# More zero matmuls before the first attention products, and the first expert's work handed out two rounds later

## The chip, the cores and the metric

The kernel runs on one core of a Trainium2 chip. The metric is the device time of one execution in microseconds (us). Engines are named as in the profile: PE is the matrix engine, PEld its weight load, DVE the vector engine, ACT the scalar engine, POOL GpSimd, SP the engine that issues most DMAs.

## What is computed

A linear attention with a decaying state gives x of 3072 tokens by 384, and a mixture of 8 experts with a balanced gate follows it.

```python
for t in range(S):                                  # B=4, H=8, S=768, D=48
    cur = einsum('bhd,bhe->bhde', u[None] * kt, vt)
    y[:, :, t] = einsum('bhd,bhde->bhe', rt, state + cur)
    state = w[None, :, :, None] * state + einsum('bhd,bhe->bhde', kt, vt)
...
logits = x @ w_gate                                 # N=3072, D=384, E=8
P = np.exp(logits - logits.max())
for _ in range(8):
    P /= P.sum(1, keepdims=True) + 1e-09
    P /= P.sum(0, keepdims=True) + 1e-09
    P *= N / E
for e in range(E):
    h = np.maximum(x @ w1[e], 0.0)                  # 384 -> 1024
    out += P[:, e:e + 1] * (h @ w2[e])              # 1024 -> 384
```

## The kernel before

**Start.** Tables of powers of the decay are made on DVE. Meanwhile PE multiplies zeros (`spin`, tile `pz`, 128x512 in fp16; nobody reads the result) and then transposes the tables (`pt_tab`). Every engine next loads a flag and branches (lines 450 and 451): if a decay lies outside a safe span, a slow path runs, a long piece of code that lies between this branch and everything that follows. Here the branch jumps over it.

**Attention rounds.** The 3072 tokens are 24 tiles of 128. A loop over rounds i = 0 to 26 writes the instructions of all engines in program order; each engine executes its own list in that order. In round i: loads for tile i+4 (SP), scaled copies `rp`, `kp` for tile i+2 (POOL, DVE), products `rk` (POOL), transposes `prT`, `pkT` of tile i+1 (PE, copied out by ACT), then `run`, then scores `pA` of tile i (PE), their masked copy `at` (DVE), the state update `pu`, `S` (PE, DVE, POOL), then `run`, then transposes `px` of tile i-2, the output `py` of tile i-1 with its scaling `x`, `xm`, `xs` (DVE, ACT), then `prepare`, and the gate products `pg` of tile i-3 with `logits` (DVE). The PSUM tiles of all of these share one tag with 4 buffers, so that `pA` of a round can start only when the `logits` or `x` of earlier tiles have been read.

**Side work.** Two lists are emptied a piece at a time between these stages. `prepare` pops one piece of `side`: expert 0's weights w1 and then w2 are split into a high and a low fp16 half, by 3 maxima (`amax`, DVE, tile `wm`), `reduce_max`, `across` (the maximum over partitions: a transpose `pmax_w` on PE, DVE's `mt_w` and `md_w`, a tiny matmul), `scale`, and 4 steps of `high` (ACT) and `low` (DVE, tile `ws`). `run(n)` calls `prepare` once and then pops n pieces of `units`. Units are expert 0's matmuls: for each of the first four tiles two `g1_chunk` (36 matmuls 128x128, tile `phc`), then four `g2_half` (12 matmuls, tile `po`). Two become available at the end of each of the rounds 2 to 5, the four `g2_half` at the end of round 5, and the next sixteen at the end of round 9. A round calls `run(1)`, `run(2 if i % 3 < 2 else 1)` and one `prepare`: so 3 pieces of side work and up to 3 or 2 units. Units then fall in rounds 3 (2), 4 (2), 5 (2), 6 (3) and 7 (3), and none is left for rounds 8 and 9.

**After.** Rounds 10 to 26, a loop over ticks that empties the rest of `units`, and 14 half experts.

Of the kernel before, what the change touches and what calls it, by code (L numbers as in the profile page):

```python
# [32 lines left out]
def rwkv_sinkhorn_moe(  # L33
# [25 lines left out]
    KC = DM // P  # L59
# [28 lines left out]
    def part(home, dtype, at, shape):  # L88

        n = 1  # L90
        for s_ in shape:
            n *= s_
        x_ = home if home.dtype == dtype else home.bitcast(dtype)
        x_ = x_[:, at : at + n]
        if len(shape) == 1:
            return x_
        names = "abcd"[: len(shape)]
        return x_.rearrange(
            f"p ({' '.join(names)}) -> p {' '.join(names)}", **{c_: s_ for c_, s_ in zip(names[1:], shape[1:])}
        )  # L100
# [21 lines left out]
    def pow2_scale(m, inv, s, down):  # L122
        V.tensor_scalar(inv, m, 1e-30, down, op0=ALU.max, op1=ALU.mult)
        V.tensor_single_scalar(
            inv.bitcast(I32), inv.bitcast(I32), EXP_MASK, op=ALU.bitwise_and
        )
        V.reciprocal(s, inv)


    def over_partitions(m, n, pool, tag, name):  # L130

        pt = pool.tile([P, TB], F32, tag=tag, name=f"pmax_{name}")
        T.transpose(pt[:n, :P], m, ident)
        mt = sm.tile([P, 1], F32, tag="mt", name=f"mt_{name}")
        V.tensor_reduce(mt[:n], pt[:n, :P], axis=AX.X, op=ALU.max)
        md = sm.tile([P, 2], F32, tag="md", name=f"md_{name}")
        V.tensor_scalar_mul(md[:n, :n], ident[:n, :n], mt[:n])
        yield pt[:, 2 * P : 2 * P + n]
        T.matmul(pt[:, 2 * P : 2 * P + n], ones[:n, :], md[:n, :n], start=True, stop=True)
        yield pt[:, 2 * P : 2 * P + n]  # L140


    def split_weights(e, r1, r2, home):
        w1h = part(home, F16, 0, (KC, F))
        w1l = part(home, F16, KC * F, (KC, F))
        w2h = part(home, F16, 2 * KC * F, (FC, DM))
        w2l = part(home, F16, 2 * KC * F + FC * DM, (FC, DM))
        isw = const.tile([P, 2], F32, name=f"isw_{e}")
        sw = sm.tile([P, 2], F32, tag="sw", name=f"sw_{e}")
        m = sm.tile([P, 2 * KC], F32, tag="wm", name=f"wm_{e}")  # L150
        ma_ = [sm.tile([P, 1], F32, tag=f"wma{j}", name=f"wma_{e}_{j}") for j in range(2)]
        res = {}
        pieces = []
        for raw, wh, wl, j in ((r1, w1h, w1l, 0), (r2, w2h, w2l, 1)):
            fl = [x.rearrange("p c f -> p (c f)") for x in (raw, wh, wl)]
            n = fl[0].shape[1] // KC

            def amax(i, fl=fl, j=j, n=n):
                V.tensor_reduce(
                    m[:, j * KC + i : j * KC + i + 1], fl[0][:, i * n : (i + 1) * n],  # L160
                    axis=AX.X, op=ALU.max, apply_absolute_value=True,
                )

            def reduce_max(j=j):
                V.tensor_reduce(ma_[j], m[:, j * KC : (j + 1) * KC], axis=AX.X, op=ALU.max)

            def across(j=j):
                res[j] = over_partitions(ma_[j], 1, ps1, "ph", f"w{e}_{j}")
                next(res[j])

            def scale(j=j):
                pow2_scale(next(res[j]), isw[:, j : j + 1], sw[:, j : j + 1], 0.25)

            def high(i, fl=fl, j=j, n=n):
                sl = slice(i * n, (i + 1) * n)
                S_.activation(fl[1][:, sl], fl[0][:, sl], AF.Copy, scale=sw[:, j : j + 1])

            def low(i, fl=fl, j=j, n=n):
                sl = slice(i * n, (i + 1) * n)
                V.scalar_tensor_tensor(  # L180
                    fl[2][:, sl], fl[0][:, sl], sw[:, j : j + 1], fl[1][:, sl],
                    op0=ALU.mult, op1=ALU.subtract,
                )

            steps = [lambda i=i, f=amax: f(i) for i in range(KC)] + [reduce_max, across, scale]
            for i in range(KC + 1):
                fs = [lambda i=i, f=high: f(i)] if i < KC else []
                fs += [lambda i=i, f=low: f(i - 1)] if i else []
                steps.append(lambda fs=fs: [f() for f in fs])
            pieces += steps  # L190
        return (w1h, w1l, w2h, w2l, isw), pieces
# [57 lines left out]
    def whole(gen):  # L249
        for _ in gen:  # L250
            pass
# [25 lines left out]
    def spin(n):  # L277
        pz = ps2.tile([P, TB], F32, tag="po", name="pz")
        for _ in range(n):
            T.matmul(pz, zeros[:, :P], zeros, start=True, stop=True)  # L280
# [4 lines left out]
    def load_part(tt, nm, src):  # L285
        b, c = divmod(tt, NCHB)
        t_ = ld.tile([P, H, D], F32, tag=nm + "n", name=f"{nm}n_{tt}", bufs=5 if nm == "v" else 3)
        Q.dma_start(t_, src[b, :, c * C : (c + 1) * C, :].rearrange("h t d -> t h d"))
        loads.setdefault(tt, {})[nm] = t_

    def load_chunk(tt):
        for nm, src in (("r", r), ("k", k), ("v", v)):
            load_part(tt, nm, src)
# [23 lines left out]
        xf[2].rearrange("p t (a q) -> p t a q", q=HP),  # L317
        unit[:, :1, 1:].unsqueeze(1).broadcast_to([P, TTH, 2 * KC, HP]), 0.0,
    )
    spin(16)  # L320
    wsafe = ac.tile([P, NPAIR], F32, name="wsafe")
    good = ac.tile([P, NPAIR], F32, name="good")
    V.tensor_scalar(wsafe, wt, W_MAX, W_MIN, op0=ALU.min, op1=ALU.max)
# [125 lines left out]
    with tc.high_priority():  # L449
        bad = nc.values_load(flag.bitcast(I32), min_val=0, max_val=0x3F800000)  # L450
        with tc.If(bad > 0):
            with tc.tile_pool(name="scratch", bufs=1, space=bass.MemoryType.DRAM) as scratch:
                scan_channels(scratch)

    load_part(0, "v", v)
    Q.dma_start(
        ub.rearrange("p h d -> p (h d)"),
# [19 lines left out]
    def gate_max():  # L477
        V.tensor_reduce(wgm, wg, axis=AX.XY, op=ALU.max, apply_absolute_value=True)

    def gate_across():  # L480
        res = over_partitions(wgm, 1, ps1, "ph", "wg")
        next(res)
        return res

    def gate_split(res):
        pow2_scale(next(res), iswg, swg, 0.25)
        S_.activation(wgh, wg, AF.Copy, scale=swg)
        V.scalar_tensor_tensor(wgl, wg, swg, wgh, op0=ALU.mult, op1=ALU.subtract)
# [6 lines left out]
    def prep(tt):  # L495
        ld_ = loads[tt]
        G.tensor_tensor(rp_[tt % 2][:, :, :D], ld_["r"], rt4, op=ALU.mult)
        V.tensor_tensor(kp_[tt % 3][:, :, :D], ld_["k"], kt4, op=ALU.mult)
        st[tt] = {}

    def bonus_dot(tt):
        ld_ = loads[tt]
        rk = at2.tile([P, H, D], F32, tag="rk", name=f"rk_{tt}")
        G.tensor_tensor(rk, ld_["r"], ld_["k"], op=ALU.mult)
        G.tensor_tensor(rk, rk, ub, op=ALU.mult)
        st[tt]["rk"] = rk
# [108 lines left out]
    def prepare():  # L615
        if side:
            side.pop(0)()

    def run(n):
        prepare()  # L620
        for _ in range(n):
            if units:
                units.pop(0)()

    W, side = split_weights(0, *raws, ws1)
    prep(0)
    prep(1)
    stage_b(0)
    bonus_dot(0)
    for i in range(NTT + 3):  # L630
        if i == 2:
            gate_max()
        if i == 3:
            gate_split(gate_res)
        if i + 2 < NTT:
            if i + 4 < NTT:
                load_chunk(i + 4)
            if i == 0:
                Q.dma_start(raws[1], w2[0].rearrange("(c p) d -> p c d", p=P))
            prep(i + 2)  # L640
        if i + 1 < NTT:
            bonus_dot(i + 1)
            stage_b(i + 1)
        run(1)
        if i < NTT:
            bonus(i)
            if ("S", i) in st:
                st[i]["S"] = st.pop(("S", i))
            stage_c(i)
        run(2 if i % 3 < 2 else 1)  # L650
        if i == 2:
            gate_res = gate_across()
        if 2 <= i <= NTT + 1:
            stage_e(i - 2)
        if 1 <= i <= NTT:
            stage_d(i - 1)
        prepare()
        if 3 <= i:
            stage_f(i - 3)
        done = i - 2  # L660
        if 0 <= done < TPB:
            units += [lambda t=done, g=g: g1_chunk(t, g, W) for g in range(2)]
            if done == TPB - 1:
                units += [lambda t=t: whole(g2_half(0, t, 0, W)) for t in range(TPB)]
                pend = [(0, t, 1) for t in range(TPB)]
        elif TPB <= done < NTT and done % TPB == TPB - 1:
            tb = done // TPB
            for j in range(2):
                g1 = [lambda fc=fc, tb=tb: g1_unit(tb, fc, W) for fc in range(j * FHC, (j + 1) * FHC)]
                g2 = [lambda a=a: whole(g2_half(*a, W)) for a in pend]  # L670
                units += merged(g1, g2)
                pend = [(tb, t, j) for t in range(TPB)]
# [448 lines left out]
    for s in range(NS):  # L1121
        tasks = stage_tasks(s)
        for g in range(NG):
            for j in range(2):
                for n, nxt in enumerate(g1_slots(s, g, j)):
# [3 lines left out]
                    i = j * NPR + n  # L1129
# [37 lines left out]
```

## Time and profile before

| | us |
|---|---|
| median of 3 runs | 1611.08 |
| the runs | 1612.73, 1610.4, 1611.08 |
| the profiled execution | 1613.47 |
| its span, first to last instruction | 1611.8 |
| PE busy in the span | 1569.0 (97%) |

The page gives one execution. A share of busy time is a mean over stages, so the stretch that the change touches, the first 117 us, is read by itself: in windows (busy time of each engine in given stretches), in the timeline (each engine's instructions in order, with what ended an idle time) and in the list of waits. Rounds are told apart by PE's `prT`, with which PE begins one: round 1 at 24.31, 2 at 31.20, 3 at 40.44, 4 at 57.47, 5 at 67.84, 6 at 78.60, 7 at 90.98, 8 at 102.17, 9 at 109.39, 10 at 116.55 us.

### The profile page before, as it was taken

To read this page: it belongs to the slowest core of one execution; us is meant where nothing else is said; L and a number is where in the kernel's file an instruction comes from. 1 tells how busy PE (TensorE), PEld (TensorE's weight loads), DVE (VectorE), ACT (ScalarE), POOL (GpSimd) and SP (SyncE) were. 2 spreads that over 40 slices of the span, in tenths; PEclk is the share of its full clock that TensorE was granted. 3 is DMA by queue.
4 is the path that set the end of the run, shared out by engine and by line. 5 is a ranking of instruction groups with operands and counts; after the bars stand their busy time and mean duration, and the time that the engine had idled before them with its cause. 6 is when DMAs were issued, how large, how long until landed. Compare 5 with 4: busy or idle time off the path is not lost.

```text
span 1611.8 us, 24273 instructions
## 1 busy us (share of the span) xinstructions
PE 1569.0 (97%) x9438; PEld 906.7 (56%) x9438; DVE 1019.6 (63%) x1706; ACT 665.9 (41%) x1174; POOL 580.1 (36%) x688
## 2 busy tenths in 40 slices
PE   7899999789999999999999999999999999999998
PEld 5887777344455555555555555555555555555555
DVE  6665554787766666666666666666666665656554
ACT  3232232243444445453545454444444443535320
POOL 7455542665020242424242424333232424242200
PEclk7999999889999999999999999999999999999999
DMA  7242320202022556565665656564545454545433
GB/s 183 50 90 64 85 60 31 74 35 84 30 93 55 103 74 122 84 123 83 113 99 75 122 80 127 84 113 56 97 52 98 55 95 54 97 55 89 60 90 130
DMA packets 159547, 135.54 MB, mean 84 GB/s; under 512 B 83906, under 2 KB 153667, under 8 KB 159427
## 3 DMA queue, kind: packets, MB, share of 16 engines
q0 software_dynamic: 44928, 61.36, 29.6%
q1 hardware_dynamic: 114288, 72.58, 15.6%
q8 instruction: 75, 1.23, 0.3%
q14 instruction: 46, 0.37, 0.1%
q10 hardware_dynamic: 210, 0.00, 0.0%
HBM read 53.69 MB, written 80.22 MB: 83 GB/s over the span
## 4 chain that ended last, share of the span: by engine, by line
PE 92%; DVE 5%; POOL 1%; issue 0%; ACT 0%; DMA 0%; SPq 0%; DVEq 0%; POOLq 0%
PE po L29 46%; PE bZ L29 11%; PE bY L29 11%; PE bB L29 4%; PE bA L29 4%; PE ph L29 4%; PE py L29 3%; PE bC L29 2%; PE pA L29 2%; PE pu L29 1%; PE phc L29 1%; DVE xv L29 1%; PE prT L29 1%; DVE ws L29 1%; PE pkT L29 1%; DVE hb L29 1%
## 5 line engine op out<-in xcount | busy, mean ns | idle before, releaser
L29 PE MATMUL po<-ws,hb 128*128 128x384 f16 x4608 | 893.9, 327 | 1.2 <-DVE cs L29 1.2
L29 PEld LDWEIGHTS <-hb 128*128 128x128 f16 x4824 | 459.7, 98 | 383.9 <-issue 5.2
L29 POOL DMA_DIRECT2D accd<-stg x288 | 250.4, 870 | 699.9 <-ACT stg L29 681.5
L29 PEld LDWEIGHTS <-ws 128*128 128x128 f16 x3168 | 300.3, 99 | 255.7 <-issue 7.6
L29 ACT ACTIVATE hb<-tb 128x512 f16<-128x512 f32 x224 | 141.1, 630 | 442.7 <-DVE tb L29 442.7
L29 DVE TENSOR_TENSOR tb<-bY,tb 128x512 f32<-128x512 f32 x168 | 116.2, 692 | 194.3 <-PE bY L29 194.3
L29 ACT ACTIVATE stg<-po,pe 128x384 f32<-128x384 f32 x312 | 179.4, 575 | 128.4 <-PE po L29 102.8
L29 PE MATMUL bZ<-xv,ws 128*128 128x512 f16 x840 | 227.0, 379 | 0.2
L29 PE MATMUL bY<-xv,ws 128*128 128x512 f16 x840 | 227.0, 379 | 0.1
L29 DVE TENSOR_TENSOR tb<-bZ,tb 128x512 f32<-128x512 f32 x168 | 115.6, 688 | 134.1 <-PE bZ L29 134.1
L29 DVE SCALAR_TENSOR_TENSOR hb<-tb,hb 128x512 f16<-128x512 f32 x224 | 155.1, 692 | 48.8 <-ACT hb L29 39.0
L29 DVE TENSOR_TENSOR tb<-bB,tb 128x512 f32<-128x512 f32 x112 | 77.5, 692 | 49.7 <-PE bB L29 47.8
L29 POOL TENSOR_TENSOR ucb<-rawb 128x256 f32<-128x256 f32 x84 | 75.7, 951 | 79.1 <-DVE tb L29 67.8
L29 PE MATMUL bA<-xv,ws 128*128 128x512 f16 x336 | 90.8, 379 | 1.0 <-ACT tb L29 1.0
L29 PE MATMUL bB<-xv,ws 128*128 128x512 f16 x336 | 90.8, 379 | 0.0
L29 PE MATMUL ph<-hb,ws 128*128 128x512 f16 x360 | 87.4, 389 | 0.0
L29 DVE SCALAR_TENSOR_TENSOR hb<-ph,hb 128x512 f16<-128x512 f32 x40 | 27.6, 689 | 60.4 <-ACT hb L29 60.3
L29 ACT COPY tb<-bZ 128x512 f32<-128x512 f32 x56 | 32.8, 586 | 68.1 <-PE bZ L29 68.1
L29 POOL TENSOR_TENSOR av<-vn,dg 128x384 f32<-128x384 f32 x24 | 19.9, 830 | 106.8 <-DVE dg L29 106.8
L29 ACT COPY stg<-po 128x384 f32<-128x384 f32 x48 | 23.0, 480 | 72.6 <-PE po L29 39.6
L29 ACT ACTIVATE xsc<-x,xs 128x384 f32<-128x384 f32 x24 | 14.8, 615 | 92.2 <-DVE xs L29 92.2
L29 DVE SCALAR_TENSOR_TENSOR ws<-ucb,sw,ws 128x768 f16<-128x768 f32 (+1 forms) x56 | 51.7, 943 | 0.0
(161 smaller groups left out, 1570.0 us busy)
## 6 DMA issues: line engine op xcount, KB each, us to landing
accd<-stg POOLq DMA_DIRECT2D x288, 192.0 KB, 3.6
rawb<-in_moe_w_dram SPq DMA_DIRECT2D x28, 768.0 KB, 6.7
e0d<-stg SPq DMA_DIRECT2D x48, 192.0 KB, 2.0
hb<-e0d SPq DMA_DIRECT2D x48, 192.0 KB, 3.5
rn<-in_r_dram SPq DMA_DIRECT2D x24, 192.0 KB, 3.5
kn<-in_k_dram SPq DMA_DIRECT2D x24, 192.0 KB, 3.7
vn<-in_v_dram SPq DMA_DIRECT2D x24, 192.0 KB, 2.8
accd<-stg SPq DMA_DIRECT2D x24, 192.0 KB, 1.8
```

Source lines behind the costliest of these rows:

```text
L29: return lambda *a, **k: self.tc.keep_in_program_order(f(*a, **k))
```

## The change

Four edits. The zeros before `pt_tab` go from 16 matmuls to 25. Eight more are written behind the branch, ahead of the first `prT`. `steps` gets two empty pieces (`rest_`), one on each side of `across`, and in rounds 3 to 7 `prepare` is called once more. And `run` hands out no unit in rounds 0 to 4; in round 5 it hands out two.

```diff
--- before.py
+++ after.py
@@ -151,6 +151,10 @@
         ma_ = [sm.tile([P, 1], F32, tag=f"wma{j}", name=f"wma_{e}_{j}") for j in range(2)]
         res = {}
         pieces = []
+
+        def rest_():
+            pass
+
         for raw, wh, wl, j in ((r1, w1h, w1l, 0), (r2, w2h, w2l, 1)):
             fl = [x.rearrange("p c f -> p (c f)") for x in (raw, wh, wl)]
             n = fl[0].shape[1] // KC
@@ -182,7 +186,7 @@
                     op0=ALU.mult, op1=ALU.subtract,
                 )
 
-            steps = [lambda i=i, f=amax: f(i) for i in range(KC)] + [reduce_max, across, scale]
+            steps = [lambda i=i, f=amax: f(i) for i in range(KC)] + [reduce_max, rest_, across, rest_, scale]
             for i in range(KC + 1):
                 fs = [lambda i=i, f=high: f(i)] if i < KC else []
                 fs += [lambda i=i, f=low: f(i - 1)] if i else []
@@ -317,7 +321,7 @@
         xf[2].rearrange("p t (a q) -> p t a q", q=HP),
         unit[:, :1, 1:].unsqueeze(1).broadcast_to([P, TTH, 2 * KC, HP]), 0.0,
     )
-    spin(16)
+    spin(25)
     wsafe = ac.tile([P, NPAIR], F32, name="wsafe")
     good = ac.tile([P, NPAIR], F32, name="good")
     V.tensor_scalar(wsafe, wt, W_MAX, W_MIN, op0=ALU.min, op1=ALU.max)
@@ -452,6 +456,7 @@
             with tc.tile_pool(name="scratch", bufs=1, space=bass.MemoryType.DRAM) as scratch:
                 scan_channels(scratch)
 
+    spin(8)
     load_part(0, "v", v)
     Q.dma_start(
         ub.rearrange("p h d -> p (h d)"),
@@ -641,13 +646,13 @@
         if i + 1 < NTT:
             bonus_dot(i + 1)
             stage_b(i + 1)
-        run(1)
+        run(i > 4)
         if i < NTT:
             bonus(i)
             if ("S", i) in st:
                 st[i]["S"] = st.pop(("S", i))
             stage_c(i)
-        run(2 if i % 3 < 2 else 1)
+        run(0 if i < 5 else 2 if i % 3 < 2 else 1)
         if i == 2:
             gate_res = gate_across()
         if 2 <= i <= NTT + 1:
@@ -655,6 +660,8 @@
         if 1 <= i <= NTT:
             stage_d(i - 1)
         prepare()
+        if 3 <= i < 8:
+            prepare()
         if 3 <= i:
             stage_f(i - 3)
         done = i - 2
```

So expert 0's w1 pieces fall in rounds 0 to 3 as before (the three lows all in round 3), the w2 pieces in rounds 3 to 6, and the twelve units in rounds 5 (2), 6 (3), 7 (3), 8 (2) and 9 (2).

The order of the instructions on PE and on DVE shows this in three places. First, PE just behind the branch, ahead of round 0 (`prT` and `pkT` are the first transposes). Before:

```order
L451 UNCONDITIONAL_BRANCH x2
L29 MATMUL prT_3813<-ident,rp_180 128x128 x4
L29 MATMUL pkT_3820<-ident,kp_182 128x128 x4
L29 MATMUL prT_3842<-ident,rp_181 128x128 x4
L29 MATMUL pkT_3849<-ident,kp_183 128x128 x4
```

Now (the two rows of zeros come eight times, then `prT`):

```order
L394 REGISTER_ALU
L394 COMPARE_AND_BRANCH
L394 UNCONDITIONAL_BRANCH
L455 UNCONDITIONAL_BRANCH x2
L29 LDWEIGHTS zeros
L29 MATMUL pz<-zeros 128x512
```

The zeros stand behind the branch, ahead of every product of the attention.

Second, PE at the end of round 1, where w1's maximum crosses partitions (`py` is tile 0's output). Before:

```order
L29 MATMUL pu_3926<-vn_3788,kp_183 128x96 x4
L29 MATMUL pmax_w_0_3934<-ident,wma_0_3807 1x128
L29 MATMUL py_3940<-vn_3778,at_185 128x48 x8
L29 MATMUL pmax_w_0_3934<-md_w_0_3938,ones 128x1
L29 MATMUL prT_3975<-ident,rp_181 128x128 x4
L29 MATMUL pkT_3982<-ident,kp_182 128x128 x4
```

Now the end of round 1, and round 2 behind its `pu`:

```order
L29 MATMUL pu_3944<-vn_3806,kp_192 128x96 x4
L29 MATMUL py_3952<-vn_3796,at_194 128x48 x8
L29 MATMUL pmax_w_0_3971<-ident,wma_0_3825 1x128
L29 MATMUL prT_3989<-ident,rp_190 128x128 x4
L29 MATMUL pkT_3996<-ident,kp_191 128x128 x4
```

```order
L29 MATMUL pu_4020<-vn_3813,kp_193 128x96 x4
L29 MATMUL pmax_w_0_3971<-md_w_0_3975,ones 128x1
L29 MATMUL pmax_wg<-ident,wgm 1x128
L29 MATMUL px_4038<-ident,xsc_3969 128x128 x3
L29 MATMUL py_4044<-S_3897,rT_3865 128x96 x4
```

The transpose `pmax_w` has moved behind `py`, and the tiny matmul that needs DVE's answer has moved half a round on, behind `pu`.

Third, DVE in round 3 (`ws` are the lows of w1, `wm` a maximum of w2, `hb_75<-phc` a unit's eviction, `at` the masked scores). Before, from the end of round 2:

```order
L29 RECIPROCAL xs_4046<-inv_s 128x1
L29 SCALAR_TENSOR_TENSOR ws_77<-ws_76,sw_3805,ws_77 128x1024
L29 TENSOR_SCALAR iswg<-pmax_wg 128x1
L29 TENSOR_SCALAR iswg<-iswg 128x1
L29 RECIPROCAL swg<-iswg 128x1
L29 SCALAR_TENSOR_TENSOR wgl<-wg,swg,wgh 128x24
L29 TENSOR_TENSOR kp_184<-kn_3885,ktab 128x8x48
L29 SCALAR_TENSOR_TENSOR ws_77<-ws_76,sw_3805,ws_77 128x1024
L29 SCALAR_TENSOR_TENSOR hb_75<-phc_0_4086,hb_75 128x4x128
L29 TENSOR_REDUCE dg_4125<-rk_3972 128x8
```

Now round 3, its middle and its end:

```order
L29 RECIPROCAL swg<-iswg 128x1
L29 SCALAR_TENSOR_TENSOR wgl<-wg,swg,wgh 128x24
L29 TENSOR_TENSOR kp_193<-kn_3903,ktab 128x8x48
L29 SCALAR_TENSOR_TENSOR ws_77<-ws_76,sw_3823,ws_77 128x1024
L29 TENSOR_REDUCE dg_4101<-rk_3986 128x8
L29 COPY_PREDICATED at_195<-mask,pA_0_4106 128x4x128
L29 COPY_PREDICATED at_195<-mask,pA_1_4107 128x4x128
L29 TENSOR_TENSOR S_4123<-pu_4118,S_4025 128x384
L29 SCALAR_TENSOR_TENSOR ws_77<-ws_76,sw_3823,ws_77 128x1024
L29 TENSOR_TENSOR hb_72<-px_4128,hb_72 128x384
```

```order
L29 RECIPROCAL xs_4151<-inv_s 128x1
L29 SCALAR_TENSOR_TENSOR ws_77<-ws_76,sw_3823,ws_77 128x1024
L29 TENSOR_REDUCE wm_3824<-ws_76 128x1
L29 TENSOR_SCALAR logits<-pg_4159,inv_s,iswg 128x8
L29 TENSOR_TENSOR kp_191<-kn_3980,ktab 128x8x48
```

The three lows stand in round 3 among the attention's own work, and no unit's eviction is left there.

## Rows read from the trace of the kernel before

**Rows 1.** The page, busy time of each engine and the clock in 40 slices
```profile
PE 1569.0 (97%) x9438; PEld 906.7 (56%) x9438; DVE 1019.6 (63%) x1706; ACT 665.9 (41%) x1174; POOL 580.1 (36%) x688
...
PEclk7999999889999999999999999999999999999999
```

**Rows 2.** Windows of rounds: us; busy PE, PEld, DVE, ACT, POOL (instructions); granted clock, DMA, GB/s
```profile
24.31:31.20 6.89, 5.70 (x54) 5.11 (x53) 6.82 (x14) 1.08 (x2) 5.43 (x6) 0.93 1.04 195
31.20:40.44 9.24, 9.24 (x63) 8.59 (x62) 7.26 (x18) 4.14 (x6) 7.95 (x8) 0.68 1.01 266
40.44:57.47 17.03, 12.64 (x141) 11.87 (x141) 10.76 (x21) 4.49 (x8) 7.85 (x9) 0.80 0.18 36
57.47:67.84 10.37, 10.37 (x148) 10.12 (x144) 8.56 (x18) 3.04 (x6) 4.72 (x6) 1.00 0.30 59
...
102.17:109.39 7.22, 6.71 (x74) 6.23 (x71) 5.17 (x13) 2.05 (x4) 4.10 (x5) 1.00 0.66 166
109.39:116.55 7.16, 6.71 (x75) 6.24 (x72) 5.15 (x13) 2.06 (x4) 5.76 (x7) 1.00 0.42 84
```

**Rows 3.** Timeline of PE: start, us, instructions, idle before and who ended it
```profile
1.31 6.09 PE L29 MATMUL pz<-zeros 128*128 128x512 f16 x16 [1.31 <-DVE zeros L29]
10.55 1.94 PE L29 MATMUL pt_tab<-ident,hb 128*128 128x128 f32 x8 [3.15 <-DVE wc L29]
17.73 1.09 PE L29 MATMUL prT<-ident,rp 128*128 128x128 f32 x4 [5.24 <-DVE kp L29]
...
21.31 2.08 PE L29 MATMUL pA<-rT,kT 64*128 64x128 f32 x16
...
28.11 0.27 PE L29 MATMUL pmax_w<-ident,wma 128*1 128x128 f32 x1 [0.60 <-DVE wma L29]
...
30.68 0.58 PE L29 MATMUL pmax_w<-md_w,ones 1*128 1x1 f32 x2 [0.58 <-DVE md_w L29]
...
43.97 0.50 PE L29 MATMUL phc<-hb,ws 128*128 128x128 f16 x3 [2.15 <-DVE ws L29]
46.71 3.17 PE L29 MATMUL phc<-hb,ws 128*128 128x128 f16 x28 [2.24 <-DVE ws L29]
...
52.28 2.17 PE L29 MATMUL phc<-hb,ws 128*128 128x128 f16 x36
...
69.89 0.38 PE L29 MATMUL pmax_w<-md_w,ones 1*128 1x1 f32 x2 [0.98 <-DVE md_w L29]
...
117.46 2.10 PE L29 MATMUL ph<-hb,ws 128*128 128x512 f16 x9
```

**Rows 4.** Timeline of DVE, same columns
```profile
23.42 1.36 DVE L29 COPY_PREDICATED at<-mask,pA 128x512 f32<-128x512 int32 x2 [3.50 <-PE pA L29]
...
25.13 2.34 DVE L29 TENSOR_REDUCE wm<-ws 128x1 f32<-128x1024 f32 x2
...
37.71 1.28 DVE L29 SCALAR_TENSOR_TENSOR ws<-ws,sw,ws 128x1024 f16<-128x1024 f32 x1
...
40.24 0.56 DVE L29 TENSOR_TENSOR x<-py,av 128x384 f32<-128x384 f32 x1 [0.37 <-PE py L29]
...
41.88 2.03 DVE L29 SCALAR_TENSOR_TENSOR ws<-ws,sw,ws 128x1024 f16<-128x1024 f32 x1
...
45.37 1.28 DVE L29 SCALAR_TENSOR_TENSOR ws<-ws,sw,ws 128x1024 f16<-128x1024 f32 x1
```

**Rows 5.** Windows of the tile pz alone
```profile
1.30:6.30 5.00, 4.99 (x12) 1.00 0.82 153
```

**Rows 6.** Windows between changes of the granted clock
```profile
9.76:23.40 13.64, 7.61 (x41) 6.71 (x41) 5.11 (x11) 3.92 (x7) 8.33 (x10) 0.50 0.70 187
...
30.24:37.05 6.81, 6.37 (x35) 5.77 (x36) 5.34 (x15) 3.66 (x5) 6.34 (x7) 0.50 1.01 291
...
43.89:50.70 6.81, 4.49 (x39) 4.04 (x41) 2.47 (x8) 1.87 (x4) 0.00 (x0) 0.50 0.14 29
```

**Rows 7.** The branch's line: duration min/median/max, first and last start
```profile
L451 PEldq COMPARE_BRANCH  x1: 6249/6249/6249, 11.2 to 11.2; - x1
```

## The prediction

> **What bounds the kernel now.** I read the page first, then windows cut at the rounds of the attention, then the timelines of PE and DVE inside them. On the page the reader is to see that PE is busy 97% of the span and that its clock falls short of full in few slices, the first among them [rows 1]. All that the change moves lies before round 10 (116.55 us): from there on the same units wait in the same list as before, and PE works without a gap, so a shift of that moment goes through to the end. The sum is therefore one of 116.55 us, and 0.2% of the time, 3.2 us, is about what a measurement can tell from no change.
>
> The windows show three kinds of rounds. Round 4, with two units, takes 10.37 us and PE is busy in all of it; DVE is busy for 8.56 [rows 2]. Round 3 has the same content on PE and takes 17.03. Rounds 8 and 9 have no units, take 7.22 and 7.16, and PE is busy for 6.71 of each [rows 2]. In rounds 1 and 2 DVE is the full engine (6.82 of 6.89 us) and then PE at a low clock (9.24 of 9.24, granted clock 0.68). The timeline says what round 3 waits for: two idle times of 2.15 and 2.24 us ended by DVE's lows of w1, and 28 matmuls that take 3.17 us where 36 later take 2.17 [rows 3]. The low clock is visible directly: 0.50 of full (the 1.2 GHz level) from 9.76 to 23.40, from 30.24 to 37.05 and from 43.89 to 50.70 us [rows 6]. PE stood idle before each: 3.15 us up to 10.55, 0.60 and 0.58 around 28 to 30.7, 2.15 up to 43.97 [rows 3].
>
> **The change, part by part.** Sums are against the profiled execution, 1613.47 us, which lies 2.4 above the median of 1611.08.
>
> (a) Nine more zeros ahead of the tables. The sixteen end at 7.40 and the tables' transposes start at 10.55, when DVE has made them [rows 3]. Twelve zeros take 5.00 us in the first window, 0.417 each [rows 5] (the row prints a clock of 1.00 there, but 512 columns in 0.417 us is the 1.2 GHz level), so nine take at most 3.75 and run into the gap of 3.15: 0 to +0.6 us. With a higher clock the transposes (1.94 us) could take half; who would gain sits in the branch behind them until 17.4 (below). I take 0.
>
> (b) Eight zeros behind the branch. At 0.417 each they are 3.3 us. Here two rows speak differently. The timeline puts PE's idle time of 5.24 us before the first transpose down to DVE's `kp` [rows 3]; by that the zeros would fit into idle time, at no cost. The branch's own row says that PE's sequencer was in the branch from 11.2 for 6.249 us, to 17.4 [rows 7], and the transpose starts at 17.73: by that the zeros, which stand behind the branch, begin no earlier than 17.4 and push the transposes to about 21.1. I take the second, since the zeros can't be issued before the branch ends. The Trainium skill ("Runtime: NRT & Kernel Launch", section "Instruction fetch mechanics") has a rule that speaks against the edit: a taken branch to code that is not in the engine's small window stalls until that page has been fetched. By it the wait is PE's own and the zeros come after it; this trace's 6.249 us agrees, and the sum is 1.7 us higher than by the timeline's releaser.
> What do they give back? The clock rose at 23.4, and the work from 17.73 to the first masked copy at 23.42 [rows 4], 5.7 us, was done at half rate. If the clock rises at the same moment, 2.3 us of that work are done by 23.4 and the other 3.4 take 1.7: `at` starts at 25.1, which is +1.7. Ends: the whole 3.3 as delay; and at the full level throughout (0.23 per 512 columns from nine in 2.10 us [rows 3]), 17.7 + 1.9 + 2.85 = 22.4, which is -1.0. I take +1.7.
>
> (c) w1's maximum spread out. PE no longer stands before `pmax_w` for 0.60 and 0.58 us [rows 3], and one low of 1.28 us leaves round 2 on DVE [rows 4]. If the clock then holds in round 2, DVE sets the pace of rounds 1 and 2: 6.82 + 7.26 - 1.28 = 12.8 us of work, and some 0.4 waiting for `py`, as before the `x` at 40.24 [rows 2, 4], against 16.13: -2.9. If the clock falls all the same, PE's 9.24 us in round 2 stay: 0. What is late next is DVE itself. I take -2.9.
>
> (d) Round 3 without units: its two waits and the low clock in front of the units go, 17.03 - 10.37 = -6.7. The wait of 0.98 us for w2's maximum in round 5 [rows 3] goes too: -1.0.
>
> (e) But rounds 3 and 4 have no cover now. PE's own work there is 10.37 less two units of 2.1, or 6.2 us. DVE has 5.17 us of attention work per round (round 8) [rows 2], in round 3 all three lows (1.28 + 2.03 + 1.28) and a maximum (2.34 for two): 10.9; in round 4 two maxima: 7.5. Masked scores, `x` and `logits` all come from DVE, and `pA` needs the buffers that these free, so PE goes at DVE's pace: +4.7 and +1.3, +6.0. If the lows slide into round 2's slack it is less, +4; if POOL and DVE get in each other's way more often (a low took 2.03 instead of 1.28 us), +7.
>
> (f) The four units now run in rounds 8 and 9, beside what PE waits for there: 7.22 + 7.16 - 2 x 6.2 = -2.0. At least the 0.51 us per round that PE wasn't busy is filled: -1.0.
>
> (g) The clock in rounds 3 and 4. PE has 6.2 us of work in 10.9 and 7.5, with gaps of two or three microseconds ahead of `py` and `pA`; gaps of 2.15 and 2.24 us are what stood at the fall at 43.9. Two of the three stretches at 0.50 last 6.8 us [rows 6]; the work of one costs up to 3.4 us if PE sets the pace, and about half of it where PE would otherwise wait for DVE. I take two stretches at 1.7: +3.4; ends 0 and 6.8.
>
> Sum: 0 + 1.7 - 2.9 - 6.7 - 1.0 + 6.0 - 2.0 + 3.4 = -1.5. Taken from the profiled execution that is 1612.0 us, from the median 1609.6. The profiled one is the slow end of the three runs, and a low-clock stretch that it had and the median lacked can't be won twice, so I stay between and near the median: **1610.4 us**, no change that a measurement can tell.
>
> **The rivals.** *Faster: the clock holds.* The zeros bring the rise forward so that (b) is -1.0, and PE's gaps in rounds 3 and 4 are too short for a fall, (g) = 0: the sum is -7.6, 1603.5 us. Bounded by (e) at its upper end it is -6.6, 1604.5. For it: granted clock 1.00 in rounds 8 and 9, where PE was idle half a microsecond per round [rows 2]. Against: the gaps here are four times that, and gaps of 2 us at 41.8 to 46.7 stood in a fall.
>
> *Slower: starved rounds at half clock.* The mechanism is (g) at its price where PE paces: at 0.50, PE's 6.2 us per round become 12.4, which is more than DVE's 10.9 and 7.5; PE then becomes the pace of rounds 3 and 4, each window of it late, and the first units of round 5 begin at half rate as well. With (g) = 6.8 and the zeros at their full 3.3 the sum is +3.5: 1614.6 us. It decides when more than two stretches at 0.50 fall between 37 and 75 us. For it: PE at 0.68 in round 2 with only short gaps. Against: rises have come after one stretch of steady work, and a PE at half rate has no gaps.
>
> *The deferral does nothing.* The units fill rounds 8 and 9 but round 3's excess is not theirs: DVE's lows are late by themselves and round 3 keeps 17.03 - 4.2 = 12.8 us, (e) being +6.6 there. The sum is then +0.4, inside no change.
>
> **How the numbers follow.** No change, 0.58 (the sum, its neighbours and the third rival); faster, 0.24; slower, 0.18. The rivals' times, 1604.5 and 1614.6, lie with their cases about the ends; the range 1605.0 to 1615.0 leaves out the rest of each.
>
> **What would show it right or wrong.** In the changed kernel: the first `prT` at about 21 us behind eight `pz` that begin near 17.5; no idle time before `pmax_w` in round 1; `phc` first in round 5 with no wait for `ws`; DVE busy nearly throughout rounds 2 to 4 and PE waiting there for DVE; a clock of 0.50 somewhere between 37 and 75 us; rounds 8 and 9 at 10 us with PE full; round 10's first `ph` within 3 us of 117.46. Wrong would be: the zeros ending before 18 us, one long stretch at full clock from 25 us on (faster), or a round 5 that begins later than 65 us (slower).

## The result and the profile after

The changed kernel takes 1614.26 us (median of 22 runs, 1610.21 to 1616.92) where the kernel before takes 1611.86 (22 runs, 1609.75 to 1613.76): a ratio of 1.0014, interval [1.0007, 1.0020], or about 2.3 us slower. That lies inside the range of the prediction and under the 3.2 us it set as its bound for no change; but with 22 runs a side the interval excludes 1, and the forecast had the sign the other way (a sum of -1.5).

The changed kernel's profiled execution took 1613.91 us, 0.4 more than that of before. Two executions are not two medians: the one of before was near the upper end of its runs, and a later part of the program, the same in both, ran 2.0 us shorter in the one of after (last section). What the change touches ends where round 10 begins, at 118.97 us now and at 116.55 before [rows 2]: +2.42 us.

The page of the changed kernel; the second line is PE's clock in 40 slices, whose second slice (about 40 to 81 us) stands at 7:

```profile
PE 1573.2 (98%) x9455; PEld 909.6 (56%) x9455; DVE 1018.3 (63%) x1706; ACT 665.1 (41%) x1174; POOL 580.6 (36%) x688
...
PEclk9799999999999999999999999999999999999999
```

Windows cut at the beginnings of rounds 1 to 10, the first from tile 0's transposes (ahead of round 0) on, to be held against [rows 2]: stretch, us, busy of PE, PEld, DVE, ACT, POOL (instructions), granted clock, DMA share, GB/s:

```profile
19.93:23.83 3.90, 3.90 (x41) 3.61 (x40) 1.79 (x4) 2.05 (x4) 3.14 (x4) 1.00 0.87 238
23.83:29.15 5.32, 5.07 (x51) 4.58 (x50) 5.32 (x9) 1.08 (x2) 5.16 (x6) 1.00 1.07 203
29.15:37.68 8.53, 7.40 (x64) 6.71 (x65) 7.16 (x22) 2.05 (x4) 8.29 (x10) 1.00 0.92 249
37.68:49.63 11.95, 9.08 (x69) 8.48 (x69) 7.71 (x18) 5.26 (x8) 8.79 (x9) 0.76 0.49 98
49.63:62.28 12.65, 12.40 (x75) 11.56 (x71) 9.43 (x17) 2.06 (x4) 6.49 (x7) 0.50 0.24 47
62.28:75.06 12.78, 12.46 (x141) 11.88 (x138) 6.58 (x17) 3.14 (x6) 4.74 (x5) 0.79 0.24 47
75.06:87.33 12.27, 12.27 (x182) 12.03 (x180) 9.41 (x20) 6.75 (x10) 5.26 (x5) 1.00 0.26 51
87.33:98.70 11.37, 11.37 (x174) 11.13 (x171) 8.13 (x16) 3.64 (x7) 6.18 (x7) 1.00 0.27 53
98.70:108.84 10.14, 10.14 (x99) 8.31 (x96) 5.07 (x13) 2.82 (x6) 5.73 (x6) 1.00 0.30 60
108.84:118.97 10.13, 10.13 (x99) 8.30 (x95) 5.03 (x13) 2.82 (x6) 5.73 (x6) 1.00 0.41 98
```

Rounds 8 and 9 do what was forecast: 10.14 and 10.13 us, PE full. Rounds 1 and 2 run at full clock and are shorter than before. Round 4 is the one to look at. It has no units, so PE's work is 6.2 us at full clock by the prediction; PE is busy for 12.40 of 12.65, more than any other engine, and the clock is 0.50 from end to end. Round 5, with its two units, takes 12.78 us, at 0.79.

The windows between changes of the clock show where this begins and ends, same columns:

```profile
13.07:19.89 6.82, 3.30 (x8) 1.25 (x9) 2.22 (x4) 0.00 (x0) 2.22 (x3) 0.50 0.61 195
19.89:43.78 23.89, 20.06 (x189) 17.95 (x187) 18.72 (x45) 9.73 (x17) 19.69 (x21) 1.00 0.95 221
43.79:67.67 23.88, 23.23 (x143) 22.08 (x144) 15.36 (x31) 4.34 (x9) 12.17 (x12) 0.50 0.26 51
67.68:118.00 50.32, 50.00 (x609) 45.60 (x607) 31.55 (x66) 17.59 (x32) 26.81 (x28) 1.00 0.27 56
```

Before, three stretches of 13.64, 6.81 and 6.81 us stood at 0.50 [rows 6]. The start and round 2 have lost 13.6 us of low clock, and the last stretch has become one of 23.88 us, over rounds 3, 4 and 5. The timeline of PE, with the idle time before a group in brackets, shows what stood there:

```profile
1.31 7.99 PE L29 MATMUL pz<-zeros 128*128 128x512 f16 x25 [1.31 <-DVE zeros L29]
10.06 1.07 PE L29 MATMUL pt_tab<-ident,hb 128*128 128x128 f32 x8 [0.77 <-DVE wc L29]
16.59 3.50 PE L29 MATMUL pz<-zeros 128*128 128x512 f16 x8 [5.46 <-PEq L455]
19.93 0.60 PE L29 MATMUL prT<-ident,rp 128*128 128x128 f32 x4
...
28.62 0.27 PE L29 MATMUL pmax_w<-ident,wma 128*1 128x128 f32 x1
...
41.62 1.13 PE L29 MATMUL pu<-vn,kp 128*128 128x96 f32 x8 [1.75 <-ACT rT L29]
...
44.20 2.02 PE L29 MATMUL py<-S,rT 128*128 128x96 f32 x8 [1.12 <-DVE at L29]
46.01 3.54 PE L29 MATMUL py<-vn,at 128*128 128x48 f32 x16
...
52.55 2.08 PE L29 MATMUL pA<-rT,kT 64*128 64x128 f32 x14 [0.24 <-ACT rT L29]
...
58.66 3.54 PE L29 MATMUL py<-vn,at 128*128 128x48 f32 x16
...
64.23 3.82 PE L29 MATMUL phc<-hb,ws 128*128 128x128 f16 x36
...
69.47 2.17 PE L29 MATMUL phc<-hb,ws 128*128 128x128 f16 x36 [0.32 <-DVE hb L29]
...
119.88 2.11 PE L29 MATMUL ph<-hb,ws 128*128 128x512 f16 x9
```

In round 3 PE waits 1.75 us for `rT` and 1.12 for `at`, and the clock falls in the second wait. From 44.20 on PE hardly waits any more: it is at half rate, and the sixteen `py` take 3.54 us in rounds 3 and 4. The first unit, at 64.23, begins at half rate too (3.82 us for 36 products where the next 36 take 2.17), and the clock is back 3.4 us after it began. DVE's timeline says from the other side who is late:

```profile
22.96 1.38 DVE L29 COPY_PREDICATED at<-mask,pA 128x512 f32<-128x512 int32 x2 [2.11 <-PE pA L29]
...
49.59 0.56 DVE L29 TENSOR_TENSOR x<-py,av 128x384 f32<-128x384 f32 x1 [2.55 <-PE py L29]
...
62.23 0.56 DVE L29 TENSOR_TENSOR x<-py,av 128x384 f32<-128x384 f32 x1 [3.09 <-PE py L29]
```

DVE waits 2.55 and 3.09 us for `py` at the ends of rounds 3 and 4; before, at the same place of round 2, it was 0.37 [rows 4].

The branch's own row stands as before [rows 7], with 5.749 us in place of 6.249:

```profile
L455 PEldq COMPARE_BRANCH  x1: 5749/5749/5749, 10.7 to 10.7; - x1
```

It ends at 16.5 and the eight zeros begin at 16.59, with an idle time that the timeline this time gives to PE's own sequencer.

### The profile page after: what moved, and what is told of

Same layout as the page of the kernel before. It is cut to its first block, busy times and chain, and to the rows that moved or that the text cites. A ratio compares the mean times of both kernels' runs of the same rounds, so it can differ in the third digit from the quotient of the medians.

```text
span 1612.2 us, 24302 instructions
## 1 busy us (share of the span) xinstructions
PE 1573.2 (98%) x9455; PEld 909.6 (56%) x9455; DVE 1018.3 (63%) x1706; ACT 665.1 (41%) x1174; POOL 580.6 (36%) x688
## 4 chain that ended last, share of the span: by engine, by line
PE 92%; DVE 5%; ACT 0%; POOL 0%; issue 0%; DMA 0%; DVEq 0%; ACTq 0%; POOLq 0%
PE po L29 45%; PE bZ L29 11%; PE bY L29 11%; PE bB L29 4%; PE bA L29 4%; PE py L29 4%; PE ph L29 3%; PE bC L29 2%; PE pA L29 1%; DVE xv L29 1%; PE pu L29 1%; PE phc L29 1%; DVE hb L29 1%; PE prT L29 1%; PE pkT L29 1%; DVE ws L29 1%
## 5 line engine op out<-in xcount | busy, mean ns | idle before, releaser
L29 DVE TENSOR_TENSOR tb<-bB,tb 128x512 f32<-128x512 f32 x112 | 77.5, 692 | 49.3 <-PE bB L29 47.4
L29 POOL TENSOR_TENSOR av<-vn,dg 128x384 f32<-128x384 f32 x24 | 19.9, 831 | 109.4 <-DVE dg L29 109.4
```

The lines of the kernel that those rows point to most:

```text
L29: return lambda *a, **k: self.tc.keep_in_program_order(f(*a, **k))
```

## The experiments

Three theories, by the letters that the expectations use. **C**: with the units gone, rounds 3 and 4 run at half clock with PE as the pace, and that is the loss; the zeros are harmless or a help. **Z**: the eight zeros behind the branch hold up all that follows, and that is the loss. **D**: DVE sets the pace of rounds 3 and 4 whatever the clock does. A fourth, P, belongs to one run and is told there. All times by ratio are against the kernel before on the same chip (medians 1611.38 to 1611.86), 0.1% being 1.6 us; a single ratio is good to about 1.5 us, the difference of two to about 2. "Round 10" is its first `prT` in the profiled execution (116.55 before, 118.97 after); that column and the one of the clock come from one execution of each kernel, the times from 9 to 22.

| run | median us | ratio [95%] | clock 0.50 after 25 us, until 120 | round 10 |
|---|---|---|---|---|
| the change | 1614.26 | 1.0014 [1.0007, 1.0020] | 43.8-67.7 | 118.97 |
| e1_zeros_alone | 1612.16 | 1.0004 [0.9995, 1.0013] | 30.8-34.2, 44.5-47.9 | 114.1 |
| e2_no_eight | 1612.49 | 1.0003 [0.9993, 1.0012] | 41.8-65.7 | 117.5 |
| e3_zeros_r34 | 1611.08 | 0.9994 [0.9984, 1.0004] | 42.4-45.8 | 114.8 |
| e4_defer_alone | 1616.02 | 1.0017 [1.0007, 1.0028] | 41.8-69.1 | 120.0 |
| e5_zeros_r34_no8 | 1609.31 | 0.9986 [0.9978, 0.9995] | 39.8-43.2 | 112.1 |
| e6_two_per_round | 1608.30 | 0.9981 [0.9973, 0.9990] | 40.5-50.7 | 111.6 |
| e7_zeros_r4 | 1614.30 | 1.0022 [1.0013, 1.0032] | 44.7-58.3 | 119.0 |
| e8_two_zeros_r3 | 1607.93 | 0.9971 [0.9961, 0.9982] | 33.9-44.1 | 113.5 |
| e9_25_alone | 1612.07 | 1.0000 [0.9991, 1.0009] | 30.4-33.8, 44.0-47.4 | 113.1 |
| e10_two_16 | 1608.66 | 0.9979 [0.9970, 0.9987] | 42.1-52.3 | 112.6 |
| e11_two_no_rests | 1611.51 | 1.0001 [0.9993, 1.0010] | 40.4-54.0 | 113.8 |
| e12_two_gate_later | 1608.55 | 0.9980 [0.9970, 0.9989] | 43.1-53.4 | 112.8 |

### Which part loses

**e1_zeros_alone**: the kernel before, with the zeros of the change and nothing else.

```diff
-    spin(16)
+    spin(25)
...
+    spin(8)
     load_part(0, "v", v)
```

> The kernel before with the zeros alone (25 and 8), units and side work untouched. Theory C (the clock stays at its lower level through the rounds without units, and that is what the change pays): the zeros only bring forward the rise at the start, round 3 begins 1 to 3 us earlier than 40.44, its units keep PE dense, and the time is 1 to 3 us below that of the kernel before. Theory Z (the eight zeros behind the branch are the loss): 1.5 to 3 us above the kernel before.

Measured: 1.0004, no change. Neither theory's number: the zeros alone neither gain what C allowed them nor lose what Z asked.

**e2_no_eight**: the changed kernel without the eight zeros behind the branch.

```diff
-    spin(8)
     load_part(0, "v", v)
```

> The changed kernel without the eight zeros behind the branch. Theory C: the first transposes run at the lower clock until about 23 us, the low stretch of rounds 3 to 5 stays, and the time is that of the changed kernel, within 1.5 us. Theory Z: it comes down by 1.5 to 3 us, to the kernel before or below it.

Measured: 1.0003, which is 1.8 us under the change; the first masked copy starts at 21.64 us, not 22.96. That is the size of Z, though a difference good to about 2 us. But the long stretch stays, as C says:

```profile
41.80:65.70 23.90, 22.64 (x137) 21.14 (x135) 16.30 (x33) 5.29 (x10) 12.36 (x12) 0.50 0.28 55
```

**e4_defer_alone**: the kernel before, with the units moved as in the change, no zeros added and w1's maximum not spread.

```diff
-        run(1)
+        run(i > 4)
...
-        run(2 if i % 3 < 2 else 1)
+        run(0 if i < 5 else 2 if i % 3 < 2 else 1)
```

> The kernel before with the units handed out as in the changed kernel, and nothing else: 16 zeros, no empty pieces, three pieces of side work per round. Theory C: a low stretch of 20 us or more from round 3 to round 5 as in the changed kernel, without what its zeros win at the start: 3 to 6 us above the kernel before. Theory P (the empty pieces and the extra piece crowd DVE in rounds 3 and 4): no slower than the kernel before, since DVE has no more to do there than before.

Measured: 1.0017, +2.7 us (interval +1.1 to +4.5): moving the units alone makes the kernel slower, by a little less than the 3 us that C asked for at least, and P falls. Round 10 begins at 120.0. Its window at 0.50, and its round 4, in the columns of above:

```profile
41.80:69.00 27.20, 25.01 (x149) 23.30 (x149) 16.52 (x35) 4.11 (x8) 12.65 (x13) 0.50 0.33 66
...
50.70:63.60 12.90, 12.66 (x76) 11.74 (x74) 7.64 (x16) 2.05 (x4) 5.74 (x6) 0.50 0.23 46
```

PE is busy for 12.66 of round 4's 12.90 us, DVE for 7.64. So the long stretch belongs to the moved units and to neither the zeros nor the maximum.

### Is it the clock, or DVE's pace?

**e3_zeros_r34**: the changed kernel with zeros at two places each in rounds 3 and 4, where the units had stood; their results go nowhere.

```diff
             stage_c(i)
+        if i in (3, 4):
+            spin(8 if i == 3 else 5)
         run(0 if i < 5 else 2 if i % 3 < 2 else 1)
...
             stage_d(i - 1)
+        if i in (3, 4):
+            spin(8 if i == 3 else 5)
         prepare()
```

> The changed kernel with two groups of zeros in each of the rounds 3 and 4, 8 and 8, 5 and 5 matmuls, where PE waits for DVE. Theory C: granted clock 1.00 from round 3 to round 5, round 5 begins near 58 us instead of 62.28 and the time falls by 3 to 5 us below the changed kernel, so below the kernel before. Theory D (DVE's pace in rounds 3 and 4 is the loss, the clock only follows): the clock is full, but the time stays within 1.5 us of the changed kernel or rises.

Measured: 0.9994, 3.2 us under the change, although PE has 26 matmuls more. Its rounds 3, 4 and 5, as windows:

```profile
38.20:51.40 13.20, 11.45 (x84) 8.48 (x85) 9.38 (x23) 5.37 (x8) 9.59 (x10) 0.87 0.40 80
51.40:60.70 9.30, 9.00 (x86) 7.33 (x82) 8.93 (x13) 2.17 (x4) 4.59 (x5) 1.00 0.27 54
60.70:70.90 10.20, 9.88 (x141) 9.57 (x138) 5.85 (x16) 3.14 (x6) 5.83 (x7) 1.00 0.30 59
```

Two of the four groups of zeros in rounds 3 and 4 on PE's timeline, the first eight begun at half rate:

```profile
43.79 2.90 PE L29 MATMUL pz<-zeros 128*128 128x512 f16 x8
...
54.79 1.24 PE L29 MATMUL pz<-zeros 128*128 128x512 f16 x5
```

Round 4 takes 9.30 us in place of 12.65 at the full clock, and round 5 10.20 in place of 12.78. DVE's work in round 4 is much the same (8.93 us busy here, 9.43 in the change). D falls for the changed kernel: PE's rate set the pace there. With the clock up DVE is close behind, 8.93 of 9.30 us. Round 3 pays for its sixteen zeros (13.20 against 11.95), eight of them begun at half rate. C had asked for more than came: full clock from round 3 on and round 5 near 58 us; the clock still fell once, for 3.4 us, and round 5 began at 60.7.

**e5_zeros_r34_no8**: e3 without the eight zeros behind the branch.

```diff
-    spin(8)
     load_part(0, "v", v)
```

> Zeros in rounds 3 and 4 as in the run before, and none behind the branch. If the loss of the changed kernel is the low clock of rounds 3 to 5 (some 3 us) and the eight zeros (some 1.5 us), each by itself, the two add up: 1 to 3 us below the kernel before. If the eight zeros were not on the path and their removal gained by chance: as with zeros in rounds 3 and 4 alone, about the kernel before.

Measured: 0.9986, 1.3 us under e3 by ratio and 2.3 under the kernel before. The two losses add up, as far as differences good to about 2 us can tell.

**e7_zeros_r4**: the changed kernel with ten zeros at each of the two places in round 4 alone.

```diff
+    G1, G2 = {4: 10}, {4: 10}
...
             stage_c(i)
+        if i in G1:
+            spin(G1[i])
...
             stage_d(i - 1)
+        if i in G2:
+            spin(G2[i])
```

> The changed kernel with zeros in round 4 alone, twice ten. Theory C: the clock still falls in round 3, near 44 us, but the low stretch ends in round 4, by 60 us, instead of at 67.7, and round 10 begins 1 to 3 us before 118.97. If the clock comes back with the time that PE has been busy, and not with the kind of work, twenty zeros change nothing about 67.7 and the time rises by 1 to 3 us.

Measured: 1.0022, no better than the change. The clock is back at 58.33 us, while the first ten run and 9.3 us sooner than in the change; the time isn't. The stretch at 0.50, as a window:

```profile
44.69:58.33 13.64, 13.40 (x70) 11.44 (x71) 11.05 (x19) 1.72 (x4) 7.97 (x9) 0.50 0.22 44
```

And the zeros on PE's timeline:

```profile
56.58 3.20 PE L29 MATMUL pz<-zeros 128*128 128x512 f16 x10
...
62.55 2.32 PE L29 MATMUL pz<-zeros 128*128 128x512 f16 x10
```

By then PE was the late engine and had no idle time to put them in, so the 5.52 us of zeros stood on its path and ate what the clock gave back. C was right on the clock and wrong on the time. In e3 the zeros of round 3 kept the clock from falling for long; here they could only bring it back.

### Useful work in place of zeros

**e6_two_per_round**: the changed kernel without the eight zeros, and the units two per round from round 4 on (the change has none in round 4).

```diff
-        run(i > 4)
+        run(i > 3)
...
-        run(0 if i < 5 else 2 if i % 3 < 2 else 1)
+        run(0 if i < 4 else 1 if i < 10 else 2 if i % 3 < 2 else 1)
```

> No zeros behind the branch, and two units in each of the rounds 4 to 9 instead of none until round 5. Theory C: units are what raises the clock again; the low stretch ends in round 4, some 10 to 14 us earlier than 67.7, and the time is 1 to 3 us below the changed kernel without the eight zeros. Theory D (DVE sets the pace of rounds 3 and 4): round 4 is no shorter with PE full, and the time stays within 1 us of that kernel.

Measured: 0.9981, 3.1 us under the kernel before and 5.3 under the change by ratio: faster than both. Windows of its rounds 3, 4 and 5 and of the stretch at 0.50:

```profile
36.32:48.28 11.96, 10.10 (x70) 9.34 (x69) 7.71 (x18) 5.38 (x8) 8.85 (x9) 0.67 0.51 102
48.28:60.11 11.83, 11.61 (x146) 11.15 (x143) 10.62 (x19) 3.14 (x6) 5.55 (x7) 0.90 0.26 52
60.11:71.20 11.09, 10.04 (x142) 9.52 (x138) 6.61 (x17) 3.14 (x6) 5.68 (x6) 1.00 0.28 55
40.49:50.72 10.23, 10.12 (x59) 9.66 (x59) 7.54 (x13) 3.43 (x6) 6.69 (x6) 0.50 0.30 59
```

The first units on PE's timeline:

```profile
50.02 0.96 PE L29 MATMUL phc<-hb,ws 128*128 128x128 f16 x8
51.20 1.74 PE L29 MATMUL phc<-hb,ws 128*128 128x128 f16 x28 [0.22 <-DVE ws L29]
```

Round 4 with two units (11.83 us) is shorter than the changed kernel's round 4 with none (12.65). One fall remains, in round 3, and the clock is back at 50.7, just after the units begin, 17 us sooner than in the change. Both are more than C had asked for (the time is 3.5 us under e2); D falls here too. Against e5 (0.9986), which has zeros where this run has units, 0.9981 is no difference that these runs can tell.

**e8_two_zeros_r3**: e6 with eight zeros at each of the two places in round 3.

```diff
+    G1, G2 = {3: 8}, {3: 8}
...
             stage_c(i)
+        if i in G1:
+            spin(G1[i])
...
             stage_d(i - 1)
+        if i in G2:
+            spin(G2[i])
```

> No zeros behind the branch, two units in each of the rounds 4 to 9, and twice eight zeros in round 3. Theory C: full clock from the start of round 1 to round 10 but for one short stretch at most; round 10 begins at 111 to 114 us and the time is 2 to 4 us below the kernel before. Theory D: no better than the run without the zeros in round 3.

Measured: 0.9971; its interval overlaps that of e6, so nothing more can be said to be won. In the profiled execution the fall came in round 2, at 33.9 us, ahead of the zeros, and the rise at 44.1, also ahead of them (the first begin at 44.7).

**e12_two_gate_later**: e6 with the gate's split written behind round 3's transposes and not ahead of them, so that `pu` and `py` needn't wait there.

```diff
-        if i == 3:
-            gate_split(gate_res)
...
             stage_b(i + 1)
+        if i == 3:
+            gate_split(gate_res)
```

> The run with two units in each of the rounds 4 to 9, with the split of the gate's weights in round 3 written behind that round's transposes and not ahead of them. There PE waits 1.75 us in round 3 for ACT's copies of the transposes, which stand behind the gate's split on ACT. Theory C: that wait goes, and with it one of the gaps ahead of the fall near 40 us; 0.5 to 3 us below 1608.3. If DVE sets round 3's pace whatever ACT does: within 0.5 us.

Measured: 0.9980, as e6. `pu` still waits 1.68 us for `rT` and `py` 1.81 for `at`, and the clock falls as before: the gate's split is not what makes these late. On ACT's timeline the copy of `rT` stands behind 3.85 us of idle time, here and in the change, that DVE's `xs` ends (the scaling behind round 2's `py`), and behind a high half of w1 (1.13 us).

### The smaller terms

**e9_25_alone**, the kernel before with 25 zeros:

```diff
-    spin(16)
+    spin(25)
```

**e10_two_16**, e6 with 16:

```diff
-    spin(25)
+    spin(16)
```

> The kernel before with 25 zeros instead of 16 ahead of the tables, nothing else. If these nine were free, as term (a) of the prediction has it: the first masked copy starts where it did (22.3 to 23.4 us) and the time is that of the kernel before, within 1 us. If they bring the start forward (the tables' transposes began at 10.05 us in all five runs with 25 zeros, at 10.55 in both with 16): first masked copy near 21.6 us, 0.5 to 2 us below the kernel before.

> The run with two units in each of the rounds 4 to 9, with 16 zeros ahead of the tables instead of 25. The other side of the same question: if the nine are free, 1608.3 as there, within 1 us; if they bring the start forward, 0.5 to 2 us more.

Measured: 1.0000, and 0.9979 beside e6's 0.9981. The nine zeros ahead of the tables cost nothing and gain nothing that these times can tell, in either order of the units. The start did come forward as e9's second alternative has it (first masked copy at 21.91 us), but the time did not follow.

**e11_two_no_rests**: e6 with w1's maximum not spread (no rests, and no second `prepare()`).

```diff
-            ... + [reduce_max, rest_, across, rest_, scale]
+            ... + [reduce_max, across, scale]
...
-        if 3 <= i < 8:
-            prepare()
```

> 25 zeros and two units in each of the rounds 4 to 9, with the side work as in the kernel before: no empty pieces, no extra piece. If spreading the weight maximum pays by the waits of 0.60 and 0.58 us in round 1 and by the clock behind them (term c), this is 1 to 3 us slower than with it (1608.3); if the units' place alone carries the gain, within 1 us of it.

Measured: 1.0001, 3.2 us over e6 by ratio. PE's two waits of [rows 3] are back, which the changed kernel hasn't. The last two lines are the beginnings of rounds 3 and 4:

```profile
26.43 0.27 PE L29 MATMUL pmax_w<-ident,wma 128*1 128x128 f32 x1 [0.66 <-DVE wma L29]
...
29.00 0.38 PE L29 MATMUL pmax_w<-md_w,ones 1*128 1x1 f32 x2 [0.58 <-DVE md_w L29]
...
36.34 0.66 PE L29 MATMUL prT<-ident,rp 128*128 128x128 f32 x4
...
50.20 1.09 PE L29 MATMUL prT<-ident,rp 128*128 128x128 f32 x4
```

The waits cost nothing here: round 3 begins at 36.34 us, and in e6 at 36.32. The difference comes in round 3, which takes 13.86 us in place of e6's 11.96. On DVE two lows of w1 (1.38 and 2.02 us) then stand between `x` and the masked copy, where e6 has one (1.28).

## Why the prediction was wrong

Its sum was -1.5 us. Adding the parts one by one through the runs gives +2.3: moving the units +2.7 (e4), then the 25 zeros and the spread maximum -2.2 (from e4 to e2), then the eight zeros +1.8 (from e2 to the change). Step by step:

- **(a)** nine zeros at nothing: right, as far as the times can tell (e9, e10).
- **(b)** eight zeros behind the branch, +1.7: right in size, and the choice between the two rows was right. They began at 16.59, at the end of the branch, with PE's sequencer as the releaser, and not in the idle time that the timeline gave to `kp`. As the prediction had it, they did not bring the rise of the clock forward: it came at 19.9 to 21.9 us in the four profiled runs with the eight and at 19.2 to 21.3 in the seven with 25 zeros and without the eight. The first masked copy starts at 23.3 on the mean of four profiled runs with the eight (22.96, 23.11, 23.88, 23.32) and at 21.5 on that of those seven; the times give 1.8 (the change against e2) and 1.3 (e3 against e5), each uncertain by about 2. In the kernel before's order of units the times don't show it (e1 against e9, 0.6 by ratio). Against the one execution of before the copy came 0.46 us sooner, not later: that execution had the low clock until 23.4 [rows 6], e4, with the same start, until 21.3. The Trainium skill ("Runtime: NRT & Kernel Launch", "Instruction fetch mechanics") has the rule that a taken branch to code outside the small window stalls the engine until that code is fetched. The trace agrees that the wait is in PE's own branch: 5.749 us, with the zeros behind it. That fetching is what fills it no run shows; on ACT, POOL, SP and DVE the branch of the same line took 0.045 to 0.067 us.
- **(c)** the spread maximum, -2.9: right in size (3.2 us by e11 against e6, the rests and the extra piece together), but not by the way that was told. Against the execution of before, rounds 0 to 2, from the first masked copy to round 3, took 14.72 us (37.68 - 22.96) in place of 17.02, and the clock held in round 2. But e11, with PE's waits and the low back in place, took 14.64 there (36.34 - 21.70) and e6 15.01 (36.32 - 21.31): where the clock holds in round 2, the waits cost nothing. What the spread won in that pair it won in round 3 (11.96 us against 13.86; 11.95 in the change and 13.85 in e4). That it keeps the clock up in round 2 isn't shown: the clock fell there in three of the five profiled kernels without the spread (before, e1, e9) and in one of the nine with it (e8).
- **(f)** units in rounds 8 and 9, -2.0: right. The two rounds took 5.9 us more (20.27 against 14.38) for 8.4 of units, so -2.5.
- **(d), (e), (g)** the rounds that the units left: wrong as a sum, by (g). Together with (f) they were put at -0.3 us (-7.7 + 6.0 - 2.0 + 3.4); e4 measured +2.7.

**The step that failed is (g)**, the count of "two stretches at 1.7". The prediction took the lengths seen before, 6.8 us, and charged each at half, holding that PE would otherwise wait for DVE. There came one stretch of 23.88 us, in which PE set the pace. The sign "DVE busy nearly throughout rounds 2 to 4 and PE waiting there for DVE" came out the other way in round 4: PE busy for 12.40 of 12.65 us, DVE for 9.43. In the profile, rounds 3 to 5 should have taken 31.6 us by the prediction's terms: 10.9 and 7.5 for DVE's pace, 9.8 for round 5 (67.84 to 78.60 before, less its wait), 3.4 for the clock. They took 37.38 (11.95 + 12.65 + 12.78). That makes (g) 9.2 us instead of 3.4. The other terms held: DVE was busy for 18.31 us of rounds 3 and 4 in e3 (9.38 + 8.93), where (e) had 18.4, only split otherwise between the two, and e3, whose clock is low for 3.4 us there, took 32.70 for rounds 3 to 5, near the 31.6, with its zeros. By the times (g) is 6.4, where e4 misses by 3.0, or 7.1, where e2 misses by 3.7 (-3.2 without the eight zeros; measured +0.5). Round 5 began at 62.28 us, short of the 65 that the prediction had set as its sign of slower: that sign was too far out.

The rival "starved rounds at half clock" named this mechanism and its place, and its condition was met in length, if not in number: one stretch of 23.9 us, more than two of 6.8. Two things kept it at a low chance. One was the argument that "rises have come after one stretch of steady work, and a PE at half rate has no gaps". It held in round 2 of the kernel before, where the attention's own products brought the clock back at 37.05; it failed in round 4 of the change, of e2 and of e4, where the same kinds of products, with hardly a gap from 44.20 to 64.23, did not. In each of these three it came back in the first unit, and in e3 and e7 while zeros ran. The other was that I looked at the moved units as work that costs 2.1 us wherever it stands, and as cover for waits. Before, the stretch from 43.89 to 50.70 ended within a microsecond behind one of them; that they might also be what ends such a stretch, and that none would come for two rounds, was not drawn from it. The rival's own price, +3.5, was off by its zeros, put at 3.3 where they cost 1.8; its (g) of 6.8 was about what the times gave.

"Faster: the clock holds" failed on the waits in round 3, which it called too short. "The deferral does nothing" fell with e4: its 12.8 us for round 3 lies between the 11.95 of the change and the 13.85 of e4, but it had no loss in rounds 4 and 5.

## What to carry to other kernels

Before moving matmuls out of a stretch, ask what the clock does in what is left: dense work that fills an engine's waits may be what keeps its rate up or brings it back, and a stretch at half rate is then a price of the move. An engine that reads as fully busy at half clock isn't proof that it has much to do; multiply by the granted clock first (12.40 us busy were some 6.2 of work). And price a low stretch by when the work that ended the earlier ones comes next, not by how long those were; filling it with zeros pays where the engine waits (e3), not where it is already late (e7). Useful work in the same place does as much (e6 against e5) and adds no work.

## What the runs showed of the hardware that was not expected

A busy PE didn't bring the clock back by itself: in the changed kernel it stood at 0.50 for 20 us (44.2 to 64.2) with PE busy nearly throughout, nearly all of it on f32 products of 48 to 128 columns. Yet products of the same kinds stood at the rise in round 2 of before (37.05) and in round 3 of e8 (44.1, in `pu`, behind the transposes and `pA` without a gap). None of the 31 rises before 120 us in the fourteen profiled kernels came while `py` ran. In round 4 of the change one wait of 0.24 us for `rT` falls inside `pA`; whether that, the order, or the kind of product decides wasn't tried and stays open.

Executions differ in a part that no experiment touched. Around 310 to 385 us the same code has up to three stretches at 0.50. Their windows in the kernel before and, behind them, in the changed kernel:

```profile
313.50:323.80 10.30, 5.37 (x14) 2.62 (x15) 8.40 (x16) 0.60 (x1) 10.14 (x14) 0.50 0.00 0
344.30:351.10 6.80, 5.87 (x17) 2.90 (x18) 6.63 (x14) 0.97 (x2) 3.18 (x5) 0.50 0.00 0
375.00:381.80 6.80, 5.70 (x17) 2.92 (x18) 4.58 (x9) 0.80 (x2) 6.41 (x10) 0.50 0.00 0
```
```profile
316.90:323.70 6.80, 3.05 (x8) 1.17 (x9) 6.66 (x13) 0.00 (x0) 6.80 (x9) 0.50 0.01 2
347.60:351.00 3.40, 3.40 (x12) 1.60 (x12) 3.37 (x6) 0.00 (x0) 1.05 (x2) 0.50 0.00 0
378.30:381.70 3.40, 3.40 (x13) 1.56 (x12) 2.69 (x5) 0.00 (x0) 3.30 (x4) 0.50 0.02 5
```

They sum to 23.9 and 13.6 us, and from round 10 to the end the two executions took 1496.9 (1613.47 - 116.55) and 1494.9 us. The profiled runs of e3, e5 and e9, with 27 us of it, took 1497.2 to 1497.9; e10's, with 13.6, took 1493.5. Executions of one kernel differ as well: of the 35 of the kernel before that were timed beside e1, the nine with a mean granted clock of 0.983 or 0.984 took 1612.2 to 1614.8 us, the five with 0.989 or 0.990 took 1609.1 to 1610.5. So a profiled time can be 2 or 3 us off its kernel's median without the code having changed, and the moment at which round 10 begins is the better measure of such a change. What decides how long these stretches last stays open.

With 25 zeros the tables' transposes came 0.5 us sooner (10.04 to 10.06 us in all eleven such runs, 10.54 or 10.55 with 16), although they stand behind more zeros. PE then left the branch sooner too: where no zeros stand behind it, the first transposes began at 15.94 to 16.60 us with 25 and at 16.94 to 17.73 with 16, and the first masked copy at 21.5 and 22.6 on the mean. The times don't show it (e9, e10).
